# One level of Strassen for the output projection of seven token chunks, with the waves in 64-column halves

## The chip, the cores and the metric

The kernel runs on one core of one Trainium2 chip. The metric is the device time of one execution in microseconds, lower is better. One launch computes everything; inputs and outputs are float32 in HBM (the two sketches and the three weight matrices may also arrive as 64-bit floats seen as pairs of 32-bit words, which the kernel narrows itself; in this case they do).

## The reference

Two stages follow each other. The first is linear attention with a polynomial sketch: q and k are projected by two 8-row sketches and the outer product of the two projections gives 64 features. The second is a gated feed-forward block over all 4352 tokens.

```python
def phi(x):                                # x: (4, 4, 1088, 32)
    a = np.einsum('rd,bhsd->bhsr', S1, x)
    b = np.einsum('rd,bhsd->bhsr', S2, x)
    return np.einsum('bhsi,bhsj->bhsij', a, b).reshape(*x.shape[:-1], r * r)
q_p, k_p = (phi(q), phi(k))
kv = np.einsum('bhsf,bhsd->bhfd', k_p, v)
z = np.sum(k_p, axis=2)
num = np.einsum('bhsf,bhfd->bhsd', q_p, kv)
den = np.einsum('bhsf,bhf->bhs', q_p, z)[..., None] + 1e-06
x = (num / den)                            # brought to (4352, 128)
gate = 1.0 / (1.0 + np.exp(-(x @ w_gate))) # w_gate, w_val: (128, 1536)
val = x @ w_val
out = gate * val @ w_out                   # w_out: (1536, 128)
```

## The kernel before

**Layout.** The attention's result is kept transposed in `xT` (128 features by 4352 tokens). The feed-forward block goes over it in nine chunks `tok_chk` of 512 tokens, the last of 256. The 1536 inner columns are 12 blocks of 128 (`NJ`). `w_sb[:, 0]`, `[:, 1]` and `[:, 2]` hold w_gate, w_val and w_out by blocks.

**A wave.** `w1` (L345) issues one wave: for one block of one chunk, a matmul for the gate and one for the value (L357, 128x128 by 512 tokens each) into the two banks of a `wave` tile. There are two such tiles (pool `psm`). ScalarE then takes the sigmoid of the first bank (`sg`, L365), and VectorE multiplies it with the second (`g`, L381, in the inner function `glu`). For the last chunk a wave takes two blocks at once. During chunk 0 the wave also carries the steps that narrow the weights of later blocks (`narrow_w`), which use ScalarE, VectorE and GpSimd.

**The output projection.** `w2` (L307) multiplies one block of w_out with `g` (L314) and accumulates over the twelve blocks of a chunk in one PSUM bank, `acc0` or `acc1` in turn by chunk. After the last block VectorE turns the result (L324, into `o_sb`), and four or eight DMAs on the SP queue store it (L335).

**Order.** The order on TensorE, VectorE, ScalarE and GpSimd is the program's own order (a manual schedule). `slot(group, waves)` (L395) issues a group of attention work and then some waves. Each step of its loop issues the pending `glu`, then takes from the list `todo` every `w2` but the newest (two behind in the last chunk), and then issues the next wave. So in the steady state TensorE sees a wave, one w_out matmul, a wave, and so on. A chunk's waves begin only when its tokens are ready (`moe["ready"]`).

**Attention work.** Batch 0 is computed at the start. For batches 1 to 3 the loop at the end spreads the work over slots:

- `turn_k`, `turn_q` (L420 on): VectorE transposes of k and q.
- `begin`: the pending `glu`, then `kps` (projections of k, `kab`), `qcomp` (projections of q into a `wave` tile, `cqps`, copied by ScalarE to `cq`) and `spread`. The last writes `cq` to DRAM on the SP queue and fetches it back, spread over partitions, by six DMAs on GpSimd's queue (L627).
- `outer` (L535), `sum_z` (L711): VectorE products and sums of the features of k.
- `kv_all`: the matmuls of `kv` (L677, L686) and ScalarE's copy. Then `qmult` and `weights_z` on VectorE, `ndt` (L732, a transpose of the kv matrix on TensorE), and `parts`: `den_j`, `den_i` for the denominators, `dn` for the numerators (L861), and the division on VectorE.
- `masks` for batch 1: small tensors, partly on GpSimd.

Waves 0 to 11 belong to chunk 0, 12 to 23 to chunk 1, and so on. `begin(1)` comes ahead of wave 13, `begin(2)` ahead of wave 29 and `begin(3)` ahead of wave 50.

**Buffers.** `raw` has six tiles under the tag `w_in` for the incoming weights. `sbG` has six `g` and three `sg` tiles. `KP` has two buffers. `den_i` uses whichever accumulator bank isn't in use.

Of the kernel before, what the change touches and what calls it, by code (L numbers as in the profile page):

```python
# [8 lines left out]
F32 = mybir.dt.float32  # L9
# [3 lines left out]
ALU = mybir.AluOpType  # L13
# [3 lines left out]
P = 128  # L17
# [3 lines left out]
def kernel(  # L21
# [12 lines left out]
    nc = tc.nc  # L34
# [3 lines left out]
    F = R * R  # L38
# [15 lines left out]
    sbA = ctx.enter_context(tc.tile_pool(name="sbA", bufs=2))  # L54
    raw = ctx.enter_context(tc.tile_pool(name="raw", bufs=NJ // 2))
    sbN = ctx.enter_context(tc.tile_pool(name="sbN", bufs=1))
    sbG = ctx.enter_context(tc.tile_pool(name="sbG", bufs=6))

    dram = ctx.enter_context(tc.tile_pool(name="dram", bufs=1, space=bass.MemoryType.DRAM))

# [82 lines left out]


    w_sb = const.tile([P, 3, NJ, P], F32, tag="w_sb", name="w_sb")
    w_in = {}

    def load_w_in(j0, j1):
# [153 lines left out]

    xT = const.tile([P, NTOK], F32, tag="xT")

    moe = {"sum": -1, "ci": 0, "w": 0, "ready": 0, "acc": None, "gate": None, "todo": []}

    def w2(ci, j0, jn, g):  # L307
        t0, tw = tok_chk[ci]
        if j0 == 0:
            moe["sum"] = ci  # L310
            moe["acc"] = pso.tile([P, TCH], F32, tag=f"acc{ci % 2}", name="moeout")
        for jj in range(jn):
            j = j0 + jj
            nc.tensor.matmul(  # L314
                out=moe["acc"][:, :tw],
                lhsT=w_sb[:, 2, j, :],
                rhs=g[:, jj, :tw],
                start=(j == 0),
                stop=(j == NJ - 1),
            )  # L320
        if j0 + jn == NJ:
            o_sb = sbA.tile([P, TCH // 32, 32], F32, tag="o_sb", name="o_sb")
            nt = tw // 32
            nc.vector.transpose(  # L324
                out=o_sb[:, :nt, :].rearrange("p t d -> p (t d)"), in_=moe["acc"][:, :tw]
            )
            c = t0
            while c < t0 + tw:
                b, r = divmod(c, S)
                n = min(t0 + tw - c, S - r) // 32  # L330
                u = (c - t0) // 32
                for g4 in range(4):

                    eng = nc.scalar if ci == len(tok_chk) - 1 and g4 % 2 else nc.sync
                    eng.dma_start(  # L335
                        out=bass.AP(
                            tensor=out.tensor,
                            offset=out.offset + (b * S + r // 32) * DM + 32 * g4,
                            ap=[[T * DM, 32], [DM, n], [1, 32]],
                        ),  # L340
                        in_=o_sb[32 * g4 : 32 * g4 + 32, u : u + n, :],
                    )
                c += n * 32

    def w1():  # L345

        ci = moe["ci"]
        t0, tw = tok_chk[ci]
        jn = TCH // tw
        j0 = moe["w"] * jn  # L350
        wv = psm.tile([P, 2, TCH], F32, tag="wave", name="wave")

        tp = tw // 2 if ci == 0 and j0 == 0 else tw
        for o in range(0, tw, tp):
            for which in range(2):
                for jj in range(jn):
                    nc.tensor.matmul(  # L357
                        out=wv[:, which, jj * tw + o : jj * tw + o + tp],
                        lhsT=w_sb[:, which, j0 + jj, :],
                        rhs=xT[:, t0 + o : t0 + o + tp],  # L360
                        start=True,
                        stop=True,
                    )
        sg = sbG.tile([P, TCH], F32, tag="sg", name="sg", bufs=3)
        nc.scalar.activation(out=sg, in_=wv[:, 0], func=ACTF.Sigmoid)  # L365
        if ci == 0:
            if j0 == 1:
                narrow_01(2, 3)
            if 0 < j0 < NJ - 2:
                narrow_w(j0 + 1, 3)  # L370
            narrow_w(j0 + 2, 1)
            narrow_w(j0 + 2, 2)
            if j0 < 3:
                narrow_w(j0 + 3, 0)
            if j0 > 1:
                narrow_w(j0 + 4, 0)


        def glu():
            g = sbG.tile([P, TCH], F32, tag="g", name="g")  # L380
            nc.vector.tensor_tensor(out=g, in0=wv[:, 1], in1=sg, op=MUL)  # L381
            moe["todo"].append((ci, j0, jn, g.rearrange("p (j t) -> p j t", j=jn)))

        moe["gate"] = glu
        moe["w"] += 1
        if j0 + jn == NJ:
            moe["ci"] += 1
            moe["w"] = 0
# [6 lines left out]
    def slot(group, waves):  # L395

        if group is not None:
            group()
        todo = moe["todo"]
        for _ in range(waves):  # L400
            more = moe["ci"] < len(tok_chk)
            if more and sum(tok_chk[moe["ci"]]) > moe["ready"]:
                break
            glu()


            last = moe["ci"] == len(tok_chk) - 1 and moe["w"] > 1
            lag = 3 if last else 2
            while len(todo) >= lag:
                w2(*todo.pop(0))  # L410
            if more:
                w1()
            elif not todo:
                break
            else:
                w2(*todo.pop(0))

    kT_of, qT_of = {}, {}

# [26 lines left out]
    def kps(b):  # L446
        t = ps2.tile([P, 2, 512], F32, tag="two", name="kps")
        ts = [t[:, 0], t[:, 1]]
        turns = [(g, pi) for g in range(4) for pi in range(2)]

        if b == 0:
            ts[1] = pso.tile([P, TCH], F32, tag="acc1", name="kps1")
            turns.sort(key=lambda x: x[1])
        for g, pi in turns:
            rows = slice(64 * pi, 64 * pi + 64)
            nc.tensor.matmul(  # L456
                out=ts[pi][32 * g : 32 * g + 32, : NJK * 32],
                lhsT=sk[rows, :],
                rhs=kT_of[b][rows, KBASE[g] : KBASE[g] + NJK],
                start=True,  # L460
                stop=True,
            )

        KAB[b] = sbA.tile([P, 2, NJK, 32], F32, tag="kab", name="kab")
        for pi in range(2):
            nc.vector.transpose(
                out=KAB[b][:, pi].rearrange("p j c -> p (j c)"), in_=ts[pi][:, : NJK * 32]
            )
        KP[b] = sbA.tile([P, 2, NJK, 2, F], F32, tag="kp", name="kp")

# [251 lines left out]
    def ndt(b):  # L724
        if b == 0:
            t = pso.tile([P, TCH], F32, tag="acc0", name="ndps")
            ndps = t.rearrange("p (w x) -> p w x", w=2)
        else:
            ndps = ps2.tile([P, 2, 512], F32, tag="two", name="ndps")[:, 0].rearrange(
                "p (w x) -> p w x", w=2  # L730
            )
        nc.tensor.matmul(  # L732
            out=ndps[:, 0, :P],
            lhsT=KVD[b][:, 0].rearrange("p c f -> p (c f)"),
            rhs=ident,
            is_transpose=True,
            start=True,
            stop=True,
        )
        ND[b] = sbA.tile([P, P], F32, tag="nd", name="nd")  # L740
        nc.scalar.copy(out=ND[b], in_=ndps[:, 0, :P])  # L741

# [62 lines left out]
        nc.vector.tensor_tensor(out=PD[b], in0=t[:, :, :WD], in1=A8[b], op=MUL)  # L805


    def den_i(b):
        dps = pso.tile([P, TCH], F32, tag=f"acc{(moe['sum'] + 1) % 2}", name="deni")
        for h in range(H):  # L810
            nc.tensor.matmul(  # L811
                out=dps[32 * h : 32 * h + 32, :WD],
                lhsT=mask["head"][:, h % 2, :],
                rhs=PD[b][:, h // 2, :],
                start=True,
                stop=True,
            )
        return dps

    def turn_den(b, dps):  # L820
        nt, over = WD // 32, (W1 - WD) // 32
        dT = sbA.tile([P, nt, 32], F32, tag="dTi", name="dTi", bufs=1)
        nc.vector.transpose(out=dT.rearrange("p t c -> p (t c)"), in_=dps[:, :WD])
        RC[b] = sbA.tile([P, 2, W1 // 32, 2], F32, tag="rci", name="rci")
        for t0, t1, u0, k in ((0, nt, 0, 0), (nt, W1 // 32, nt - over, 4)):
            nc.vector.tensor_scalar_add(
                RC[b][:, :, t0:t1],
                dT[:, u0 : u0 + t1 - t0, k : k + 4].rearrange("p t (n c) -> p n t c", n=2),
                1e-6,
            )  # L830
        nc.vector.reciprocal(out=RC[b], in_=RC[b])


    def dn(b, n, mid=None, pool=(ps2, "two")):
        t0, tn = q_chk[n]
        w = 32 * tn
        if b == 0:
# [8 lines left out]
                stop=True,  # L846
            )
        if b == 0:
            dT = sbA.tile([P, 9, 32], F32, tag="dT", name="dT")
            rc = sbA.tile([P, 9, 2], F32, tag="rc", name="rc")  # L850

        def turn():
# [1 line left out]

        if mid is not None:
            mid(turn, rc, dT)
        t = pool[0].tile([P, 2, 512], F32, tag=pool[1], name="nps")
        for h in range(H):
            for c in range(2):
                rows = slice(64 * c, 64 * c + 64)  # L860
# [174 lines left out]
    def parts(b):  # L1035
        den_j(b)
        glu()
        divide1 = dn(b, 1, pool=(psm, "wave"))
        dps = den_i(b)
        divide0 = dn(b, 0)  # L1040
        turn_den(b, dps)
        divide1()
# [77 lines left out]
```

## Time and profile before

| | |
|---|---|
| median of 3 runs | 303.54 us (303.41 to 303.98) |
| span of the profiled execution | 301.7 us |
| waves, L357: 436 passes, busy | 191.6 us |
| w_out, L314: 216 passes, busy | 105.2 us |
| sigmoid, L365: 102, mean | 597 ns |
| g, L381: 102, mean | 689 ns |
| transpose of a chunk's result, L324, mean | 678 ns |
| DVE additions of 64x256, both inputs in SBUF, L711, mean | 417 ns |
| granted TensorE clock from 45 to 295 us | 1.00 |

The passes of L357 and L314 overlap in the records, so their mean durations (565 and 575 ns) are longer than the distance from one to the next, and the chain of waits is the place to read a pass's price. PE is TensorE, PEld its weight loads, DVE VectorE, ACT ScalarE, POOL GpSimd and SP the engine whose queue issues most DMAs. VectorE's busy time is uneven: 27.2 of the 40 us from 45 to 85, 31.7 of the 60 from 85 to 145, 31.2 of the 60 from 145 to 205, and 26.1 of the 90 from 205 to 295, where only the feed-forward block is left. GpSimd does nothing after 164.5 us.

### The profile page before, as it was taken

To read this page: it belongs to the slowest core of one execution; us is meant where nothing else is said; L and a number is where in the kernel's file an instruction comes from. 1 tells how busy PE (TensorE), PEld (TensorE's weight loads), DVE (VectorE), ACT (ScalarE), POOL (GpSimd) and SP (SyncE) were. 2 spreads that over 40 slices of the span, in tenths; PEclk is the share of its full clock that TensorE was granted. 3 is DMA by queue.
4 is the path that set the end of the run, shared out by engine and by line. 5 is a ranking of instruction groups with operands and counts; after the bars stand their busy time and mean duration, and the time that the engine had idled before them with its cause. 6 is when DMAs were issued, how large, how long until landed. Compare 5 with 4: busy or idle time off the path is not lost.

```text
span 301.7 us, 3642 instructions
## 1 busy us (share of the span) xinstructions
PE 295.3 (98%) x1363; PEld 137.3 (46%) x1363; DVE 154.7 (51%) x268; ACT 80.7 (27%) x150; POOL 33.0 (11%) x62
## 2 busy tenths in 40 slices
PE   8899999999999999999999999999999999999994
PEld 3444434453444444434444445344444444444683
DVE  6997789764635545383365444932232223222331
ACT  3556533222122222212232222122222222222220
POOL 1465550410000400000004000000000000000000
PEclk9999999999999999999999999999999999999999
DMA  7993440897101591350016900200020000100011
GB/s 226 358 337 89 103 144 6 201 223 192 42 15 19 136 225 35 77 187 0 0 27 168 218 17 2 36 2 0 0 32 3 0 0 12 25 0 0 9 28 18
DMA packets 30546, 24.24 MB, mean 80 GB/s; under 512 B 20480, under 2 KB 25728, under 8 KB 30528
## 3 DMA queue, kind: packets, MB, share of 16 engines
q1 hardware_dynamic: 27024, 16.15, 20.5%
q0 software_dynamic: 2592, 7.08, 10.5%
q10 hardware_dynamic: 912, 0.77, 1.0%
q8 instruction: 11, 0.18, 0.2%
q14 instruction: 7, 0.06, 0.1%
HBM read 20.73 MB, written 3.26 MB: 80 GB/s over the span
## 4 chain that ended last, share of the span: by engine, by line
PE 86%; DVE 5%; DMA 3%; issue 2%; POOL 2%; ACT 1%; SPq 0%; DVEq 0%; POOLq 0%; ACTq 0%
PE wave L357 52%; PE moeout L314 27%; DMA bq<-dq 2%; PE nps L861 2%; POOL head L118 1%; PE kvz L677 1%; DVE head L109 1%; DVE w_sb L127 1%; DVE qp L655 1%; DMA s_in<-in_S_dram 1%; PE kps L456 1%; DVE head L105 1%; PE cqps L602 0%; PE deni L811 0%; PE dps L841 0%
## 5 line engine op out<-in xcount | busy, mean ns | idle before, releaser
L357 PE MATMUL wave<-xT,w_sb 128*128 128x512 f32 (+1 forms) x436 | 191.6, 565 | 0.0
L381 DVE TENSOR_TENSOR g<-wave,sg 128x512 f32<-128x512 f32 x102 | 70.3, 689 | 131.0 <-ACT sg L365 130.7
L357 PEld LDWEIGHTS wave<-xT,w_sb 128*128 128x128 f32 x436 | 82.8, 190 | 93.0 <-issue 85.7
L365 ACT ACTIVATE sg<-wave 128x512 f32<-128x512 f32 x102 | 60.9, 597 | 197.8 <-PE wave L357 197.8
L314 PE MATMUL moeout<-g,w_sb 128*128 128x512 f32 (+1 forms) x216 | 105.2, 575 | 0.3 <-DVE w_sb L127 0.3
L314 PEld LDWEIGHTS moeout<-g,w_sb 128*128 128x128 f32 x216 | 39.9, 190 | 44.8 <-issue 38.9
L118 POOL TENSOR_TENSOR head<-head,tail 128x384 int32<-128x384 int32 (+2 forms) x14 | 13.4, 954 | 18.2 <-DVE head L109 14.0
L627 POOL DMA_DIRECT2D qp<-dq x6 | 3.5, 583 | 105.9 <-DMA dq<-cq 105.9
L535 DVE TENSOR_TENSOR kp<-kab 128x1152 f32<-128x1152 f32 (+2 forms) x10 | 10.5, 1070 | 0.0
L655 DVE TENSOR_TENSOR qp<-qp,bq 128x1152 f32<-128x1152 f32 (+1 forms) x7 | 9.0, 1288 | 0.0
L258 PE MATMUL warm<-const-float32-1.0 128*128 128x512 f32 (+1 forms) x12 | 7.1, 720 | 0.8 <-PEq L1104 0.8
L109 DVE SCALAR_TENSOR_TENSOR head<-cap,head 128x384 int32<-128x384 int32 (+2 forms) x14 | 7.5, 535 | 0.5
L127 DVE SCALAR_TENSOR_TENSOR w_sb<-square,head 128x384 f32<-128x384 f32 (+1 forms) x11 | 5.7, 518 | 3.9 <-POOL head L118 3.9
L324 DVE STREAM_TRANSPOSE o_sb<-moeout 128x512 f32<-128x512 f32 (+1 forms) x9 | 6.1, 678 | 1.4 <-PE moeout L314 1.3
L627 POOL DMA_DIRECT2D bq<-dq x12 | 6.7, 574 | 0.5 <-DVE g L381 0.2
L101 ACT ACTIVATE tail<-w_in 128x384 int32<-128x384 uint32 (+1 forms) x13 | 6.6, 521 | 0.2 <-DMA w_in<-in_moe_w_gate_dram 0.2
L97 POOL TENSOR_SCALAR cap<-w_in 128x384 f32<-128x384 f32 (+1 forms) x13 | 6.4, 502 | 0.0
L886 DVE TENSOR_TENSOR xT<-nps,rb 128x576 f32<-128x576 f32 (+2 forms) x9 | 5.9, 660 | 0.5
L861 PE MATMUL nps<-qp,nd 64*32 64x256 f32 (+1 forms) x128 | 5.5, 402 | 0.5 <-ACT nd L741 0.4
L436 DVE STREAM_TRANSPOSE qT<-kq 128x512 f32<-128x512 f32 (+1 forms) x8 | 5.7, 716 | 0.0
L117 ACT ACTIVATE square<-cap 128x384 f32<-128x384 f32 (+1 forms) x11 | 5.1, 463 | 1.8 <-DVE w_sb L127 1.7
L425 DVE STREAM_TRANSPOSE kT<-kq 128x1088 f32<-128x1088 f32 (+2 forms) x5 | 5.3, 1068 | 0.0
(89 smaller groups left out, 85.6 us busy)
## 6 DMA issues: line engine op xcount, KB each, us to landing
qp<-dq POOLq DMA_DIRECT2D x6, 576.0 KB, 7.5
bq<-dq POOLq DMA_DIRECT2D x12, 288.0 KB, 9.8
v<-in_v_dram SPq DMA_DIRECT2D x16, 144.0 KB, 4.5
kq<-in_k_dram SPq DMA_DIRECT2D x3, 544.0 KB, 3.9
kq<-in_q_dram SPq DMA_DIRECT2D x3, 544.0 KB, 4.8
w_in<-in_moe_w_out_dram SPq DMA_DIRECT2D x6, 256.0 KB, 7.2
w_in<-in_moe_w_gate_dram SPq DMA_DIRECT2D x5, 256.0 KB, 6.1
w_in<-in_moe_w_val_dram SPq DMA_DIRECT2D x5, 256.0 KB, 6.8
```

The costliest lines, as they stand in the source:

```text
L109: nc.vector.scalar_tensor_tensor(out=head, in0=cap, scalar=-0x40000000, in1=head, op0=ALU.bitwise_and, op1=ALU.bitwise_or)
L118: nc.gpsimd.tensor_tensor(out=head, in0=head, in1=tail, op=ALU.add)
L127: nc.vector.scalar_tensor_tensor(out=out, in0=square, scalar=1.265625 * 2.0**-30, in1=head, op0=ALU.is_ge, op1=MUL)
L258: nc.tensor.matmul(out=t[:, 0, :n], lhsT=x, rhs=r, start=True, stop=True)
L314: nc.tensor.matmul(out=moe["acc"][:, :tw], lhsT=w_sb[:, 2, j, :], rhs=g[:, jj, :tw], start=(j == 0), stop=(j == NJ - 1),)
L357: nc.tensor.matmul(out=wv[:, which, jj * tw + o : jj * tw + o + tp], lhsT=w_sb[:, which, j0 + jj, :], rhs=xT[:, t0 + o : t0 + o + tp], sta ...
L365: nc.scalar.activation(out=sg, in_=wv[:, 0], func=ACTF.Sigmoid)
L381: nc.vector.tensor_tensor(out=g, in0=wv[:, 1], in1=sg, op=MUL)
L535: eng.tensor_tensor(out=KP[b][:, pi, j0:j1].rearrange("p j m (i l) -> p (j m) i l", i=R), in0=bass.AP(tensor=a0.tensor, offset=a0.offset, ...
L627: get.dma_start(out=t[64 * c : 64 * c + 64 if i else P, n * H * W1 : (n + 1) * H * W1], in_=bass.AP(tensor=d0.tensor, offset=d0.offset, ap ...
L655: nc.vector.tensor_tensor(out=q0, in0=q0, in1=half(BQ[b], n), op=MUL)
L861: nc.tensor.matmul(out=t[32 * h : 32 * h + 32, c, :w], lhsT=ND[b][rows, 32 * h : 32 * h + 32], rhs=half(QP[b], n)[rows, 2 * (h % 2) + h // ...
```

## The change

Chunks 1 to 7 (`fast`) compute w_out by one level of Strassen's scheme in Winograd's form. Two contraction blocks, two halves of the 128 output columns and two halves of the 512 tokens make the 2x2 blocks, so that seven products of 64 columns by 256 tokens stand for eight. Four sums of weight blocks (`weight_sums`, once, in two parts) and four sums of token blocks (`token_sums`, for every pair of waves) are made on GpSimd. The four token sums take three instructions, of which the first makes two of them.

The products go to TensorE in two groups per pair. `w2_a` (four products, accumulated in `acc0`) is due three waves after the pair's second wave, `w2_b` (three products, in `acc1`) four waves after it. Each product writes partitions 0 to 63 or 64 to 127, and the two kinds alternate within a group. `todo` now holds such due times; chunks 0 and 8 keep `w2`, with a lag of two and three waves. At a chunk's end ScalarE copies the upper half of each bank, VectorE combines the seven sums in two and four additions, and one transpose of 64 partitions by 1024 replaces the old one.

From chunk 1 on, a wave's matmuls are cut into two 64-column halves. `ndt` for batches 1 to 3 becomes two plain matmuls with the identity, one for each column half. `den_i` moves from an accumulator bank into the unused columns of the `wave` tile that holds the numerators. `g` becomes a tile for two waves, with three buffers. `KP` and one `dT` go down to one buffer.

```diff
+    def fast(ci):
+        return 0 < ci < len(tok_chk) - 1 and tok_chk[ci][1] == TCH
+    def weight_sums(n0, n1):
+        w = w_sb[:, 2].rearrange("p (n f) d -> p f n d", f=2)[:, :, n0:n1]
+        s = ws[:, :, n0:n1]
+        a11, a12 = w[:, 0, :, :64], w[:, 1, :, :64]
+        a21, a22 = w[:, 0, :, 64:], w[:, 1, :, 64:]
+        for out, in0, in1, op in (
+            (s[:, 0], a21, a22, ALU.add),
+            (s[:, 1], s[:, 0], a11, ALU.subtract),
+            (s[:, 3], a12, s[:, 1], ALU.subtract),
+            (s[:, 2], a11, a21, ALU.subtract),
+        ):
+            nc.gpsimd.tensor_tensor(out=out, in0=in0, in1=in1, op=op)
+    def token_sums(g):
+        t = raw.tile([P, 4, HALF], F32, tag="w_in", name="tsum")
+        g1 = g[:, 0].rearrange("p (t x) -> p t x", t=2)
+        nc.gpsimd.tensor_tensor(
+            out=t[:, :2],
+            in0=g.rearrange("p f (t x) -> p t f x", t=2)[:, 1],
+            in1=g1,
+            op=ALU.subtract,
+        )
+        nc.gpsimd.tensor_tensor(out=t[:, 2], in0=t[:, 1], in1=g1[:, 0], op=ALU.add)
+        nc.gpsimd.tensor_tensor(out=t[:, 3], in0=t[:, 2], in1=g[:, 1, :HALF], op=ALU.subtract)
+        return t
...
+    def w2_a(ci, i, g, t):
+        if i == 0:
+            moe["sum"] = ci
+            fst["a"] = pso.tile([P, TCH], F32, tag="acc0", name="prod")
+        lo, hi = fst["a"][:64], fst["a"][64:]
+        w, first, last = w_sb[:, 2], i == 0, i == NJ // 2 - 1
+        product(lo[:, :HALF], w[:, 2 * i, :64], g[:, 0, :HALF], first, last)
+        product(hi[:, :HALF], w[:, 2 * i + 1, :64], g[:, 1, :HALF], first, last)
+        product(lo[:, HALF:], ws[:, 3, i], g[:, 1, HALF:], False, last)
+        product(hi[:, HALF:], ws[:, 1, i], t[:, 2], False, last)
+        if last:
+            e = fst["e"] = raw.tile([P, 2, 2, HALF], F32, tag="w_in", name="other")[:64]
+            r = fst["r"] = raw.tile([P, 5, HALF], F32, tag="w_in", name="res")[:64]
+            nc.scalar.copy(out=e[:, 0], in_=hi.rearrange("p (u x) -> p u x", u=2))
+            nc.vector.tensor_tensor(
+                out=ends(r, 1, 3), in0=twice(lo[:, :HALF]), in1=e[:, 0], op=ALU.add
+            )
+            nc.vector.tensor_tensor(out=r[:, 2], in0=lo[:, HALF:], in1=r[:, 4], op=ALU.add)
...
+    def w2_b(ci, i, g, t):
...
+        p5 = (lo[:, :HALF], ws[:, 0, i], t[:, 0], first, last)
+        p4 = (hi[:, :HALF], w[:, 2 * i + 1, 64:], t[:, 3], first, last)
+        p7 = ((hi if i % 2 else lo)[:, HALF:], ws[:, 2, i], t[:, 1], False, i >= NJ // 2 - 2)
+        for p in (p4, p5, p7) if i % 2 else (p5, p4, p7):
+            product(*p)
+        if last:
+            e, r = fst["e"], fst["r"]
+            nc.scalar.copy(out=e[:, 1], in_=hi.rearrange("p (u x) -> p u x", u=2))
+            nc.vector.tensor_tensor(out=r[:, 0], in0=lo[:, HALF:], in1=e[:, 1, 1], op=ALU.add)
+            nc.vector.tensor_tensor(out=r[:, 4], in0=r[:, 4], in1=r[:, 0], op=ALU.add)
+            nc.vector.tensor_tensor(out=r[:, 3], in0=r[:, 4], in1=e[:, 1, 0], op=ALU.subtract)
+            nc.vector.tensor_tensor(
+                out=ends(r, 2, 2), in0=twice(lo[:, :HALF]), in1=ends(r, 2, 2), op=ALU.add
+            )
+            o_sb = sbA.tile([P, 2, TCH // 32, 32], F32, tag="o_sb", name="o_sb")
+            nc.vector.transpose(
+                out=o_sb[:64].rearrange("p d t x -> p (d t x)"),
+                in_=r[:, 1:].rearrange("p u x -> p (u x)"),
+            )
+            store(ci, lambda g4: o_sb[32 * (g4 % 2) : 32 * (g4 % 2) + 32, g4 // 2])
...
     def w1():
...
+        turn = (moe["w"] // 2) % 2
         for o in range(0, tw, tp):
             for which in range(2):
                 for jj in range(jn):
...
+                    for c in (0,) if ci == 0 else (1 - turn, turn):
+                        d = slice(0, P) if ci == 0 else slice(64 * c, 64 * c + 64)
+                        nc.tensor.matmul(
+                            out=wv[d, which, jj * tw + o : jj * tw + o + tp],
+                            lhsT=w_sb[:, which, j0 + jj, d],
+                            rhs=xT[:, t0 + o : t0 + o + tp],
+                            start=True,
+                            stop=True,
+                        )
...
+            if j0 == NJ - 3:
+                weight_sums(0, NJ // 4)
+        if ci == 1 and j0 == 1:
+            weight_sums(NJ // 4, NJ // 2)
+        if moe["w"] % 2 == 0:
+            moe["g"] = sbG.tile([P, 2, TCH], F32, tag="g", name="g")
+        pair, odd, n = moe["g"], moe["w"] % 2, moe["n"]
         def glu():
-            g = sbG.tile([P, TCH], F32, tag="g", name="g")
+            g = pair[:, odd]
             nc.vector.tensor_tensor(out=g, in0=wv[:, 1], in1=sg, op=MUL)
-            moe["todo"].append((ci, j0, jn, g.rearrange("p (j t) -> p j t", j=jn)))
+            todo = moe["todo"]
+            if not fast(ci):
+                lag = 3 if ci else 2
+                part = (ci, j0, jn, g.rearrange("p (j t) -> p j t", j=jn))
+                todo.append((n + lag, lambda: w2(*part)))
+            elif odd:
+                part = (ci, j0 // 2, pair, token_sums(pair))
+                todo.append((n + 3, lambda: w2_a(*part)))
+                todo.append((n + 4, lambda: w2_b(*part)))
...
-            while len(todo) >= lag:
-                w2(*todo.pop(0))
+            while todo and todo[0][0] <= moe["n"]:
+                todo.pop(0)[1]()
             if more:
                 w1()
             elif not todo:
                 break
             else:
-                w2(*todo.pop(0))
+                todo.pop(0)[1]()
...
+        for c in range(2 if b else 0):
+            nc.tensor.matmul(
+                out=ndps[64 * c : 64 * c + 64, 0, :P],
+                lhsT=KVD[b][:, 0, c],
+                rhs=ident,
+                start=True,
+                stop=True,
+            )
...
-    def den_i(b):
-        dps = pso.tile([P, TCH], F32, tag=f"acc{(moe['sum'] + 1) % 2}", name="deni")
+    def den_i(b, t):
+        dps = t[:, 0, W1 : W1 + WD]
```

## The prediction

> **What bounds the kernel now.** I read the page's first part, then its slices, then what TensorE waits for, then the chain of waits, and only then the single groups.
>
> ```profile
> PE 295.3 (98%) x1363; PEld 137.3 (46%) x1363; DVE 154.7 (51%) x268; ACT 80.7 (27%) x150; POOL 33.0 (11%) x62
> ...
> PEclk9999999999999999999999999999999999999999
> ...
> PE 86%; DVE 5%; DMA 3%; issue 2%; POOL 2%; ACT 1%; SPq 0%; DVEq 0%; POOLq 0%; ACTq 0%
> ```
>
> Busy time of a pipelined engine proves little, so the waits of TensorE decide. This is the whole answer for that engine:
>
> ```profile
> PE warm L258 <- PEq L1104: 0.8, 1, 0.8
> PE ndps L732 <- ACT kvd L699: 0.4, 1, 0.4
> PE nps L861 <- ACT nd L741: 0.4, 1, 0.4
> PE moeout L314 <- DVE w_sb L127: 0.3, 1, 0.3
> PE gram L502 <- POOL gh L490: 0.3, 1, 0.3
> PE dps L841 <- DVE zb L525: 0.2, 1, 0.2
> PE nps L861 <- DVE qp L655: 0.2, 1, 0.2
> ```
>
> Seven waits, 2.6 us together, nearly all in the first 20 us. After that TensorE is fed without a hole: a microsecond of its work removed is a microsecond of time, and a microsecond of waiting added is one lost. Nothing stands ready to hide a new wait. The chain of waits gives the prices:
>
> ```profile
> 62.72 1.72 PE wave L357 x4
> 64.43 1.28 PE kvz L677 x72
> 65.71 0.25 PE kvz L686 x8
> 65.96 1.06 PE moeout L314 x2
> 67.02 1.72 PE wave L357 x4
> ...
> 71.42 0.86 PE moeout L314 x2
> ```
>
> A matmul is two passes here (x4 for the two matmuls of a wave, x2 for one of w_out), so a full 512-column pass costs 0.43 us and 256 columns 0.215. After an attention group the first w_out matmul takes 1.06 instead of 0.86.
>
> **What the skill says.** (1) "TensorEngine Tiling (Array Packing)", Key Properties: changing the tiling mode drains TensorE. The trace agrees: in the single records every change of shape leaves 0.09 us without a start, and into the full 128x128 shape another 0.10 between the first two passes (the 0.20 above); into a 64-column shape (denj, 64x64) the second is 0.05. (2) The same section says that tiles operate independently. The 72 passes of kvz (four 32-column tiles, 64 columns) in 1.28 us are 18 ns each, where 64 columns alone cost 54: in the records four start 7 ns apart and the next four 55 ns later, although each matmul's second pass precedes the next tile's first in program order. (3) "SBUF — State Buffer", Who interferes with whom: a VectorE instruction with two SBUF inputs contends with GpSimd's reads. The trace agrees: GpSimd's addition at 39.82 took 1.96 us under VectorE's qp at 39.56, and 1.00 elsewhere. (4) "TensorE: Matmul & The Clock Gate", Part 1: an idle window of about 3.4 us halves the clock. No gap here after 20 us is that long.
>
> **The change, part by part.**
>
> *Products.* For a pair of contraction blocks, two matmuls (1.72 us) become seven products of 64 columns by 256 tokens. Two column halves run beside each other, so seven times two passes of 0.215 over two halves is 1.505. There are 7 chunks of 6 pairs: 42 x 0.215 = 9.0 us removed. A wave in halves has the same columns per half, 1.72 as before. Weight loads of 64 columns (denj: 131 ns) lie beside passes of 215 or more.
>
> *Mode changes.* Chunk 0's last w_out between chunk 1's half waves is one more trip (0.2 + 0.15). In chunk 8, w_out is full and the waves are halves: four entries at 0.20 and three returns at 0.15, 1.25. Returns from attention groups now go to halves, 9 x 0.05 = 0.45 cheaper. Sum +1.1. A B group has three products, so one half runs 0.43 behind until the next B; a drain in that state wastes half of that: about 9 drains, half of them uneven, +0.9. The column-half ndt has two passes of 128 columns instead of one, +0.1 each. All in all +2.1: TensorE's own work falls by 6.9.
>
> *GpSimd's token sums.* The additions at L118 (1.00 us for 384 columns, 0.73 for 256) give 2.1 ns a column and 0.18 fixed; the 128-column float product at L535 (0.39) lies slightly below that line. So the three sums (512, 256, 256) cost 1.26 + 0.72 + 0.72 = 2.7 per pair, against 4.9 of TensorE: not a bound. In the steady state the sum that group A needs (t[:, 2]) is there 1.5 (sigmoid, g) + 2.0 after the odd wave, and A's fourth product comes 5.4 after it: hidden by 1.9. That cover fails where GpSimd is held up. Its queue is in order, and for each batch it waits for dq and then issues six DMAs:
>
> ```profile
> 54.52 0.75 POOL L627 DMA_DIRECT2D qp<-dq  x1 [10.11 <-DMA dq<-cq]
> 55.50 1.12 POOL L627 DMA_DIRECT2D bq<-dq  x2 [0.23 <-DVE g L381]
> 56.59 0.56 POOL L627 DMA_DIRECT2D qp<-dq  x1
> 57.10 1.14 POOL L627 DMA_DIRECT2D bq<-dq  x2
> ```
>
> Batch 1: begin(1) puts these before wave 13 (counting waves from 0). Behind them stand the second weight_sums (four sums of 192 columns, 4 x 0.59 = 2.4) and then the first token sums: 58.2 + 2.4 + 2.0 = 62.6. TensorE reaches that product early, because chunk 1's first w_out comes three waves in and nothing lies between: wave 13 starts at 52.55 (52.42 in the chain, 0.15 of mode change, rounded), three waves end at 57.7, the fourth product is due at 58.15. It waits 4.4 us, in front of everything on TensorE's queue, and nothing gives that back. Bounds: 0 if GpSimd's sums were free and passed the DMAs (the queue excludes it), 3.5 at the 0.39 row's rate, 5.8 with sum_z (1.22, 0.68, two SBUF inputs) slowing it as at 39.82. I take 4.4.
>
> Batch 2: dq's landing and the six issues end 6.9 after the group (98.06 to 104.97). The sums of waves 28 and 29 then need 2.0, and TensorE wants them at 7.7: 1.2 late (0 to 1.9). Batch 3 has an even split: its sums start after g of wave 51 and meet outer (1.35, two SBUF inputs): 0.4 (0 to 0.9).
>
> *VectorE's chunk end.* Instead of one transpose (0.71) there are, after A, additions of 0.69 and 0.42, and after B three of 0.42, one of 0.69 and a transpose of 64x1024 (1.22; the 128x1088 at L425 is 1.30): 3.2 us in one piece ahead of the next g. In chunks 5 to 7 the delayed g ends 4.7 after B and its bank is wanted at 4.9: just hidden. Beside attention work it isn't. Chunk 1's end falls ahead of begin(2): turn_k (1.30), turn_q (0.67), g, the 3.1, g, turn_q (0.77), and cqps needs that last turn at 7.3 after A and gets it at 8.8: 1.5 (0 to 2). Chunk 2's end falls ahead of qmult(2): zw and qp come late for denj and nps, 1.6 (0 to 2.5); the old kernel had no wait there. Batch 3: 0.4 (0 to 0.8). ScalarE's two copies (0.6) per chunk lie in its idle time (27% busy). The rest (kp and dT single, deni in the wave's bank, accumulators acc0 and acc1 both in use, wanted again some 4 us after their last product) comes to nothing: each buffer's last reader is done a wave earlier.
>
> *Sum.* -6.9 + 4.4 + (1.2 + 1.5 + 1.6) + (0.4 + 0.4) = +2.6. The profiled span is 301.7; the median of the runs is 303.54 (303.41 to 303.98), 1.8 above it by the time around the span, which the change leaves alone. 303.54 + 2.6 = 306.1.
>
> **Rivals.**
>
> *The waits are small, the products win* (faster). For it: the old trace has no wait beside the same attention work, and VectorE was only half busy. Against it: the in-order GpSimd queue. With the 4.4 alone it is 303.54 - 6.9 + 4.4 = 301.0; with half of that 298.8; with none 296.6. I put it at 299.
>
> *The waits eat the gain* (slower, the forecast): 306.1. It decides where GpSimd's first token sums come more than 6.9 us late in sum with VectorE's delays; its place is the first A group of chunk 1, and begin(2). With all upper bounds, 5.8 + 1.9 + 2.5 + 2 + 1.7 = 13.9, it is 310.5.
>
> *Column halves lose their overlap or the clock drops* (clearly slower). Two like halves meet at most borders between a wave and a product group. If the queue couldn't reach past the second one, each of some 84 borders would idle half the array for 0.43, 84 x 0.215 = 18: 303.54 + 2.6 + 18 = 324. The kvz records speak against it: there TensorE passes over at least three second passes. Alone, a halved clock after the wait in chunk 1 would add some 1.7 (half of 3.4), by the skill's window, an estimate.
>
> *No difference*: gain and waits cancel within 0.6.
>
> **How the numbers follow.** Faster 0.41 (around 299, 296.5 to 302.9), no difference (within 0.2%, 0.6 us, about what a measurement of this kernel can tell) 0.05, the waits eat the gain 0.48 (304.2 to 311), lost overlap 0.06 (312 to 325). So faster 0.41, same 0.05, slower 0.54. The likeliest gives 306.1. The range 297 to 311 leaves out the lost overlap and the last tenth of the good case.
>
> **What would show it.** The first w2_a products of chunk 1: a wait of TensorE on POOL of 4 to 6 us near 58 to 63, with L627's DMAs and weight_sums just ahead on POOL. Waits of cqps on DVE qT in batch 2, and of denj or nps on DVE. In late chunks, a period of two waves of 4.94 instead of 5.15 without waits: that confirms the 9.0. If that period is 5.15 or more, the overlap of halves is wrong; if no wait on POOL appears, the forecast is wrong and the time is near 297 to 299.

## The result, and the profile after

| | before | after |
|---|---|---|
| median | 303.76 us (303.41 to 304.01, 4 runs) | 319.6 us (318.57 to 321.52, 4 runs) |
| span of the profiled execution | 301.7 us | 318.3 us |
| mean granted TensorE clock in it | 1.000 | 0.972 |

The ratio is 1.0531 (95% interval 1.0493 to 1.0569): 15.8 us slower, where 2.6 had been forecast. The four executions of the changed kernel were granted 0.972, 0.984, 0.982 and 0.972 of the clock on average, so what the clock takes differs between them; the profile is of the first. From the page of the changed kernel: busy time by engine, the granted clock in 40 slices of 8 us, and the engines' shares of the chain that ended last.

```profile
PE 299.3 (94%) x2176; PEld 153.6 (48%) x2176; DVE 184.9 (58%) x310; ACT 88.8 (28%) x164; POOL 161.6 (51%) x196
...
PEclk9999999879999799995999999999999999999999
...
PE 64%; DVE 14%; POOL 10%; issue 6%; DMA 2%; ACT 2%; SPq 0%; POOLq 0%; ACTq 0%; DVEq 0%
```

Two things are new. VectorE and GpSimd are a quarter of the chain (7% before), and the clock dips in four slices: two side by side (56 to 72 us), one from 103 and one from 143 us. Next, TensorE's waits in the changed kernel: total, times, longest. The rest of that answer is the few waits of the first 20 us that the old kernel had too.

```profile
PE prod L339 <- POOL tsum L334: 6.6, 3, 5.2
PE nps L982 <- DVE qp L766: 2.3, 2, 1.2
PE cqps L713 <- DVE qT L547: 1.7, 1, 1.7
PE denj L917 <- ACT sg L465: 1.3, 1, 1.3
PE wave L457 <- DVE g L487: 0.8, 2, 0.7
```

All waits are 15.1 us, 12.5 more than before. For denj this view names the sigmoid sg, but that ended at 141.28. What ended last is VectorE's zw, at 141.82, and it stands behind the chunk end, which is one piece of 3.3 us here (start, duration, line, operation, and in brackets the idle time before it and what ended it):

```profile
136.77 0.42 DVE L429 TENSOR_TENSOR res<-prod,other 64x256 f32<-64x256 f32 x1
138.84 1.24 DVE L436 STREAM_TRANSPOSE o_sb<-res 64x1024 f32<-64x1024 f32 x1
141.60 0.22 DVE L904 TENSOR_TENSOR zw<-z,eight 128x64 f32<-128x64 f32 x1
141.93 0.62 PE L917 MATMUL denj<-b,zw 64*64 64x160 f32 x8 [1.30 <-ACT sg L465]
```

The largest wait has its cause in GpSimd's timeline:

```profile
57.58 1.14 POOL L738 DMA_DIRECT2D bq<-dq  x2
58.67 1.10 POOL L323 TENSOR_TENSOR ws<-w_sb 128x192 f32<-128x192 f32 x1
59.85 0.59 POOL L323 TENSOR_TENSOR ws<-ws,w_sb 128x192 f32<-128x192 f32 x1
60.52 0.94 POOL L323 TENSOR_TENSOR ws<-w_sb,ws 128x192 f32<-128x192 f32 x1
61.43 0.76 POOL L323 TENSOR_TENSOR ws<-w_sb 128x192 f32<-128x192 f32 x1
62.15 1.44 POOL L328 TENSOR_TENSOR tsum<-g 128x512 f32<-128x512 f32 x1
63.67 0.72 POOL L334 TENSOR_TENSOR tsum<-tsum,g 128x256 f32<-128x256 f32 x1
64.45 0.69 PE L339 MATMUL prod<-tsum,ws 128*64 128x256 f32 x1 [5.21 <-POOL tsum L334]
```

The product takes 0.69 where 0.38 is usual: TensorE comes back at half its clock. Eight stretches of the same trace show how that hangs together (stretch, length, PE busy and instructions, granted clock, DMA share, GB/s). The borders are those at which the clock changed, or 3.41 us from one:

```profile
57.88:61.29 3.41, 1.36 (x10) 1.00 0.94 221
61.29:64.71 3.42, 0.26 (x2) 0.50 1.04 241
64.71:68.12 3.41, 3.41 (x11) 0.50 1.02 224
102.25:105.67 3.42, 1.73 (x36) 1.00 0.31 47
105.67:109.08 3.41, 3.41 (x13) 0.50 0.46 121
139.80:143.21 3.41, 1.45 (x12) 1.00 0.16 23
143.21:146.62 3.41, 2.87 (x40) 0.50 0.59 109
146.62:150.04 3.42, 3.42 (x19) 0.50 0.74 275
```

After the windows at full clock in which TensorE was busy for 1.36, 1.73 and 1.45 us, the next 3.41 us run at half clock, however full they are. The window from 102.25 holds no wait longer than 1.69 us. The DMA share in the three is 0.94, 0.31 and 0.16, so it isn't what they have in common. And a window at half clock has to be fuller before the clock comes back: the one from 143.21, with 2.87 us of work, was followed by another at half clock, those with 3.41 were not.

To split the difference I add up the single matmul records: each pass streams its columns at 0.43 us for 512 (twice that at half clock), over its share of the array. "Unused" is the part of the array that is idle while another part streams. The split is a model: with each pass at full length from its recorded start, the four changes come out as -8.7, +6.4, +15.5 and +3.4, so an entry is good to about half a microsecond.

| us | before | after | change |
|---|---|---|---|
| array streaming, at full clock | 281.35 | 272.95 | -8.4 |
| added by the half clock | 0 | 6.3 | +6.3 |
| nothing streams (waits, changes of shape, ends) | 17.8 | 32.75 | +15.0 |
| array unused while streaming | 2.56 | 6.26 | +3.7 |
| span | 301.7 | 318.3 | +16.6 |

In the late chunks the products do what they were meant to do. From the chain of waits of the changed kernel, a period of two waves is 4.94 us (221.00 to 225.94; 4.96 is the mean of the fourteen up to 290.43), not 5.15:

```profile
221.00 1.72 PE wave L457 x8
222.71 0.64 PE prod L339 x5
223.36 1.72 PE wave L457 x8
225.08 0.86 PE prod L339 x6
225.94 1.77 PE wave L457 x8
```

### The profile page after: what moved, and what is told of

It reads as the page before. It is cut to its first block, busy times and chain, and to the rows that moved or that the text cites. A ratio compares the mean times of both kernels' runs of the same rounds, so it can differ in the third digit from the quotient of the medians.

```text
span 318.3 us, 5511 instructions
## 1 busy us (share of the span) xinstructions
PE 299.3 (94%) x2176; PEld 153.6 (48%) x2176; DVE 184.9 (58%) x310; ACT 88.8 (28%) x164; POOL 161.6 (51%) x196
## 3 DMA queue, kind: packets, MB, share of 16 engines
HBM read 20.73 MB, written 3.26 MB: 75 GB/s over the span
## 4 chain that ended last, share of the span: by engine, by line
PE 64%; DVE 14%; POOL 10%; issue 6%; DMA 2%; ACT 2%; SPq 0%; POOLq 0%; ACTq 0%; DVEq 0%
PE wave L457 40%; PE prod L339 16%; POOL head L118 3%; POOL tsum L328 2%; PE moeout L370 2%; POOL ws L323 2%; DVE head L109 2%; DVE g L487 2%; PE nps L982 2%; DVE w_sb L127 1%; DVE o_sb L436 1%; POOL bq L738 1%; POOL tsum L334 1%; PE kvz L788 1%; DMA dq<-cq 1%
## 5 line engine op out<-in xcount | busy, mean ns | idle before, releaser
L457 PE MATMUL wave<-xT,w_sb 128*64 128x512 f32 (+3 forms) x820 | 215.8, 577 | 0.8 <-DVE g L487 0.8
L457 PEld LDWEIGHTS wave<-xT,w_sb 128*64 128x64 f32 (+1 forms) x820 | 83.3, 143 | 71.0 <-issue 52.4
L328 POOL TENSOR_TENSOR tsum<-g 128x512 f32<-128x512 f32 x42 | 57.8, 1377 | 97.6 <-DVE g L487 97.6
L339 PE MATMUL prod<-tsum,ws 128*64 128x256 f32 x252 | 68.8, 391 | 6.6 <-POOL tsum L334 6.6
L339 PEld LDWEIGHTS prod<-tsum,ws 128*64 128x64 f32 x252 | 33.4, 140 | 21.6 <-issue 8.5
L335 POOL TENSOR_TENSOR tsum<-tsum,g 128x256 f32<-128x256 f32 x42 | 34.2, 815 | 3.3
L339 PE MATMUL prod<-g,w_sb 128*64 128x256 f32 x168 | 33.9, 382 | 0.1
L334 POOL TENSOR_TENSOR tsum<-tsum,g 128x256 f32<-128x256 f32 x42 | 31.6, 753 | 3.3
L339 PE MATMUL prod<-tsum,w_sb 128*64 128x256 f32 x84 | 26.0, 392 | 0.0
L370 PE MATMUL moeout<-g,w_sb 128*128 128x512 f32 (+1 forms) x48 | 18.9, 503 | 0.3 <-DVE w_sb L127 0.3
L370 PEld LDWEIGHTS moeout<-g,w_sb 128*128 128x128 f32 x48 | 8.5, 189 | 8.3 <-issue 4.2
```

The lines of the kernel that those rows point to most:

```text
L328: nc.gpsimd.tensor_tensor(out=t[:, :2], in0=g.rearrange("p f (t x) -> p t f x", t=2)[:, 1], in1=g1, op=ALU.subtract,)
L334: nc.gpsimd.tensor_tensor(out=t[:, 2], in0=t[:, 1], in1=g1[:, 0], op=ALU.add)
L335: nc.gpsimd.tensor_tensor(out=t[:, 3], in0=t[:, 2], in1=g[:, 1, :HALF], op=ALU.subtract)
L339: nc.tensor.matmul(out=out, lhsT=lhsT, rhs=rhs, start=start, stop=stop, skip_group_check=True)
L370: nc.tensor.matmul(out=moe["acc"][:, :tw], lhsT=w_sb[:, 2, j, :], rhs=g[:, jj, :tw], start=(j == 0), stop=(j == NJ - 1),)
L457: nc.tensor.matmul(out=wv[d, which, jj * tw + o : jj * tw + o + tp], lhsT=w_sb[:, which, j0 + jj, d], rhs=xT[:, t0 + o : t0 + o + tp], sta ...
```

## The experiments

**Theory.** The products save their 8.4 us; three things take it back and more: waits on GpSimd and VectorE (12.5), windows at half clock that those waits set off (6.3), and uneven column halves (3.7). **Rivals.** (a) Work in column halves costs by itself, whatever waits there are. (b) The waits are one thing: GpSimd's queue alone, and VectorE's chunk end would be hidden without it. (c) The clock is a by-product that costs little.

### h_halves: the halves alone

Waves and w_out of chunks 1 to 8 in 64-column halves, without Strassen products, sums and the new chunk end.

```diff
-        return 0 < ci < len(tok_chk) - 1 and tok_chk[ci][1] == TCH
+        return False
...
+            for c in (0, 1) if ci else (0,):
+                d = slice(64 * c, 64 * c + 64) if ci else slice(0, P)
                 nc.tensor.matmul(
-                    out=moe["acc"][:, :tw],
-                    lhsT=w_sb[:, 2, j, :],
+                    out=moe["acc"][d, :tw],
+                    lhsT=w_sb[:, 2, j, d],
...
-                lag = 3 if ci else 2
+                lag = 3 if ci == len(tok_chk) - 1 else 2
```

> The column halves alone: waves and w_out of chunks 1 to 8 in 64-column halves, no Strassen products, no token or weight sums, the old one-piece transpose and the old lags. Theory (the loss is waits on GpSimd and VectorE, and the halved clock that these waits bring): 303.8 to 305, no new wait of TensorE over 1 us, no halved clock between 20 and 295 us. Rival (halves themselves cost, by uneven draining or because two half-array streams let the clock fall): 308 or more, with stretches of halved clock.

Measured: 303.64 us, ratio 0.9992 (0.997 to 1.0014), a little below the range. Its page shows the full clock throughout, and its chain of waits two waves of eight half passes with the old distances:

```profile
222.84 1.72 PE wave L460 x8
224.55 0.86 PE moeout L372 x4
225.41 1.72 PE wave L460 x8
```

Rival (a) falls: two column halves overlap fully, at no cost that can be measured. Everything that is lost comes with the sums, the chunk end and the seven products.

### a_ws and a_sync: what stands ahead of the token sums on GpSimd

a_ws makes the second weight_sums a wave earlier, ahead of the six DMAs:

```diff
-        if ci == 1 and j0 == 1:
+        if ci == 1 and j0 == 0:
             weight_sums(NJ // 4, NJ // 2)
```

> The changed kernel with the second weight_sums one wave earlier, ahead of batch 1's DMAs on GpSimd's queue. Theory: TensorE's wait of 5.2 us on the first token sums of chunk 1 falls by the 3.5 us that weight_sums took there (58.67 to 62.15), to about 1.7, and the halved clock after it goes or shrinks (1.8 us more): 314 to 316. Rival (the wait comes from the DMAs alone): no change, 319 to 320. Rival (the clock falls whatever the wait): 316, with three stretches of halved clock as before.

a_sync issues the six fetches of each batch on SP's queue instead of GpSimd's:

```diff
-spread(b, (0, 1), cq[b], nc.sync, nc.gpsimd)
+spread(b, (0, 1), cq[b], nc.sync, nc.sync)
```

> The changed kernel with the six fetches of each of the batches 1 to 3 on the SP queue and not on GpSimd's. Theory: GpSimd's queue no longer stands behind dq; both waits on token sums (5.2 and 1.1 us) fall to under 1 us together, the first stretch of halved clock goes (1.8 us): 311 to 313. Rival (GpSimd is simply too slow for its sums, the DMAs don't matter): 318 or more. Risk: the fetches land later and qp's products wait longer.

Measured: a_ws 314.01 us (ratio 1.0348, 1.0319 to 1.0376), a_sync 309.25 us (1.0208, 1.0167 to 1.0249). The wait on tsum falls from 6.6 to 5.2 in all with the first and to 1.6 with the second; the waits on VectorE stay as they were. a_ws is just inside its range, a_sync is 1.75 below it, and neither wait fell as far as expected. In a_ws the wait in chunk 1 is 2.55 and not 1.7: beside VectorE's sum_z the second token sum took 1.60 instead of 0.72. The one in batch 2 grew from 0.97 to 2.21, likely because the half clock ahead of it, which had hidden a part of it, was gone (in a_warm and a_split below, where it is gone too, that wait is 1.62 and 1.42). In a_sync:

```profile
PE nps L982 <- DVE qp L766: 2.3, 2, 1.2
PE cqps L713 <- DVE qT L547: 1.7, 1, 1.7
PE prod L339 <- POOL tsum L334: 1.6, 2, 1.2
PE denj L917 <- ACT sg L465: 1.3, 1, 1.3
```

Rival (b) falls: VectorE's waits don't hang on GpSimd's queue. And a_sync gains 10.35 where its removed wait is 5.0. The rest is clock: 17.07 us of half clock have become one stretch of 3.41, and the time in which the array streams falls from 279.26 to 274.37, which is another 4.9 (a_ws too has one, behind its wait in batch 2). In a_sync, stretches as above:

```profile
96.74:100.16 3.42, 1.73 (x32) 1.00 0.47 76
130.87:134.29 3.42, 1.07 (x11) 1.00 0.24 38
134.29:137.70 3.41, 3.26 (x42) 0.50 0.43 58
```

The wait of 1.69 on cqps is in the window from 96.74 here, and the clock doesn't fall after it. In the changed kernel the same wait lay in a window that was just as busy (1.73), and it did. So the threshold is near. In each of the twelve traces the changes of clock tell where the windows lie. Every window at full clock with 1.45 us or less of busy time halved it, of four with 1.71 to 1.73 one did, and none with 1.76 or more.

Busy time counts a small tile like a full array. Count the work instead: each pass at 0.43 us for 512 columns, times the share of the 128 rows and of the 128 columns that it uses. Then the order has no overlap: every window with 1.20 us of work or less was followed by half clock, and none with 1.25 or more. The two windows on cqps are apart, with 1.20 in the changed kernel and 1.46 in a_sync. The same border fits the way back. At half clock the window from 143.21 of the changed kernel did 1.19 us of such work, and the clock stayed down; that from 134.29 in a_sync did 1.37, and it came back. This was read from the traces afterwards; no run was made to test it, and 0.05 us between the two sides is little. What falls into a window depends on where its borders lie, and those lie elsewhere in every trace.

### a_warm: the clock by itself

Twelve unused products of 64 columns by 512 tokens stand ahead of the waiting product in chunk 1, so that TensorE works while it waits. They add 5.3 us of TensorE's work and write a bank that nothing reads.

```diff
+        if ci == 1 and i == 0:
+            keep = ps2.tile([P, 2, 512], F32, tag="two", name="keep")
+            for n in range(12):
+                x = slice(64 * (n % 2), 64 * (n % 2) + 64)
+                product(keep[x, n % 2], w_sb[:, 0, n, x], xT[:, :512], True, True)
         product(hi[:, HALF:], ws[:, 1, i], t[:, 2], False, last)
```

> The changed kernel with twelve more matmuls of 64 columns by 512 (5.2 us of TensorE, results unused) ahead of the product of chunk 1 that waits for the first token sums. Theory (an idle TensorE is what halves the clock): the time of that place stays, since the products fill the wait, and the halved clock after it goes: 317 to 318.5, two stretches of halved clock and not three. Rival (the clock falls for another reason): 319.6 or more, three stretches.

Measured: 315.05 us, ratio 1.0397 (1.0353 to 1.0441): 4.5 faster than the changed kernel, with more work, and faster than expected. The page and the timeline:

```profile
PEclk9999999999999999999999999999999999999999
```

```profile
59.02 5.31 PE L339 MATMUL keep<-xT,w_sb 128*64 128x512 f32 x23
64.67 0.43 PE L339 MATMUL prod<-tsum,ws 128*64 128x256 f32 x1 [0.34 <-POOL tsum L334]
```

The product starts 0.2 us later than in the changed kernel (64.45), so the wait as such is not shortened; what is gained is clock. That all three stretches went, not just the first, was not expected. The later waits are still there (1.7 on cqps, 1.3 on denj, 2.3 on nps), but the windows lie otherwise over them. A border at 102.07 cuts the wait of cqps (101.57 to 103.26), and the windows on its two sides have 2.91 and 2.23 us of busy time, where 1.73 halved the clock in the changed kernel. A border at 139.61 comes between the waits of denj and nps in the same way (2.11 and 2.22). That is the profiled execution; the four were granted 1.000, 0.988, 0.992 and 1.000 on average (314.59, 317.72, 315.41 and 314.68 us). Rival (c) falls: the clock alone is worth 4.5 us of the 15.8, and 5 in the two executions at the full clock.

### a_split: VectorE's chunk end in three pieces

The additions and the transpose after B are cut at two points and issued after later values of g.

```diff
+    def end_1():
+        e, r, lo = fst["e"], fst["r"], fst["b"][:64]
...
+    def end_2(ci):
+        r = fst["r"]
...
+                if j0 == NJ - 1:
+                    todo.append((n + 5, end_1))
+                    todo.append((n + 6, lambda: end_2(ci)))
+                todo.sort(key=lambda x: x[0])
```

> The changed kernel with VectorE's work at a chunk's end cut in three: two additions stay with the last products, the other two come one wave later, the transpose and the store two waves later. Theory: TensorE's wait of cqps on qT in batch 2 (1.7 us) goes, those of denj and nps there (1.3 and 1.2) go or halve, and the halved clock that followed them comes less often: 312 to 316; the 5.2 us on GpSimd in chunk 1 stays. Rival (these waits come from more VectorE work as such, not from its one piece): waits as before, 319 or so.

Measured: 311.39 us, ratio 1.0254 (1.0238 to 1.027), 8.2 below the changed kernel and a little below its range. cqps waits 0.3, the wait of denj is gone, but nps, which was to gain too, takes a part of it up:

```profile
PE prod L339 <- POOL tsum L334: 6.7, 2, 5.2
PE nps L992 <- DVE qp L776: 2.8, 2, 1.7
```

The half clock in chunk 1 stays (6.83 us from 61.45), and the two later stretches are gone. Rival (b) falls here too: the waits of cqps and denj came from the chunk end standing in one piece.

### b_all and c_best: the three together, and chunk 8

b_all has the edits of a_ws, a_sync and a_split. c_best adds chunk 8's w_out in halves (the second edit of h_halves), so that the end has no changes of shape.

> The changed kernel with all three: second weight_sums one wave earlier, the fetches of batches 1 to 3 on the SP queue, VectorE's chunk end in three pieces. Theory: the products' 8.4 us come through once the waits and the halved clock are gone: 298 to 302, all waits of TensorE after 20 us under 3 us together, no halved clock. Rival (the columns saved are lost to uneven halves and mode changes too): 303 to 306.

> As b_all, and chunk 8's output projection in two column halves as well, so that TensorE keeps one mode to the end. Theory: the seven mode changes of chunk 8 (1.25 us by the prediction's prices) go: 1.0 to 1.5 below b_all, 297 to 300.5. Rival (mode changes are hidden there): the same as b_all.

Measured: b_all 303.42 us, ratio 0.9994 (0.9984 to 1.0004); c_best 302.87, ratio 0.9971 (0.9959 to 0.9982). Both miss their range on the slow side; b_all is where its rival had it. c_best is 0.55 below b_all, where the prediction's price for chunk 8's changes of shape was 1.25. In their profiled executions nothing streams at half clock any more. In c_best the streaming is 8.4 us less than before, and still almost nothing is gained: nothing streams for 22.5 us (+4.7) and 5.58 are unused (+3.0). One remaining wait, from its timeline:

```profile
56.16 2.32 POOL L328 TENSOR_TENSOR tsum<-g 128x512 f32<-128x512 f32 x1 [6.42 <-DVE g L496]
57.86 1.70 DVE L835 TENSOR_TENSOR z<-kp 128x1024 f32<-128x1024 f32 x1
58.56 1.59 POOL L334 TENSOR_TENSOR tsum<-tsum,g 128x256 f32<-128x256 f32 x1
60.20 0.43 PE L339 MATMUL prod<-tsum,ws 128*64 128x256 f32 x1 [1.19 <-POOL tsum L334]
```

With nothing ahead of them on their queue, the sums are still late: beside VectorE's outer and sum_z they take 2.32 and 1.59 instead of 1.26 and 0.72. That is 1.9 us for a cover of less than one. The cause is read from the overlap of the records; neither neighbour was moved to test it.

### d_even, d_qm and d_both: the two terms that were left

d_even keeps the products but makes the B groups even: p7 of an even pair goes with the next odd pair.

```diff
-        for p in (p4, p5, p7) if i % 2 else (p5, p4, p7):
+        if i % 2 == 0:
+            fst["p7"] = p7
+        for p in (p4, p5, p7, fst["p7"]) if i % 2 else (p5, p4):
             product(*p)
```

> The best version so far (weight sums, fetches, chunk end in pieces, chunk 8 in halves), with w2_b in even groups: an even pair issues p5 and p4 only, the next odd pair p4, p5 and both p7, two products for each column half. The same products are computed. Theory: the 3 us of TensorE's array that stay unused while it streams come from the odd third product, which leaves one half 0.43 us behind until the next w2_b, so that each of the some 70 changes of shape and waits beside attention work drains uneven halves. Then unused falls from about 5.6 to 3.5 or below, and the time from 302.9 to 300.5 to 301.5. Rival: the unevenness comes from the waits and from reordering across halves whatever the groups; then unused stays above 5 and the time at 302.5 to 303.

d_qm issues qmult one slot earlier:

```diff
+        qmult(b, 0)
         slot(lambda: kv_all(b), wn)
...
-        qmult(b, 0)
         weights_z(b)
-        slot(lambda: ndt(b), 1)
         qmult(b, 1)
+        slot(lambda: ndt(b), 1)
```

> The best version so far, with qmult of both halves one slot earlier (the first ahead of kv_all's slot, the second ahead of ndt's), so that qp is ready when nps asks for it. Theory: the two waits of nps on qp (1.8 in batch 2 and 1.2 in batch 3) are VectorE being late, not work of TensorE, and they are lost time: both go, and the time falls by 2 to 3, to 300 to 301. Rival: VectorE is late in this stretch by the sum of its work beside GpSimd's sums, so another wait takes the place (denj on zw, or a wave on g): the time falls by less than 1, to 302 to 303.

d_both has the two together.

> Both edits together: even groups in w2_b and qmult one slot earlier. Theory: the gains add, as the one is columns left unused and the other waits: 298 to 300. Rival: waits at the same borders absorb each other and it is within 0.5 of the better of the two.

Measured against 303.58 us of the kernel before: d_even 301.07 (ratio 0.9914, 0.9897 to 0.993), d_qm 301.34 (0.9929, 0.991 to 0.9949), d_both 299.85 (0.9865, 0.9832 to 0.9898). In d_even the unused array falls from 5.58 to 4.15 and the span by 1.7. The time is in its range, the unused array is not (3.5 or below): the odd group is a part of it, not the whole. In d_qm the waits of nps are gone (2.8), but a wave now waits 0.9 for g, which the rival had as its sign. The time fell by 1.5, between the 2 to 3 of the theory and the 1 of the rival. d_both, the waits of its TensorE above 0.8 us:

```profile
PE prod L339 <- POOL tsum L334: 1.2, 1, 1.2
PE wave L468 <- DVE g L498: 1.0, 1, 1.0
```

The gains add (1.8 and 1.5 against c_best, 3.0 together). d_both is inside its range and beats both kernels: -8.4 streaming, +3.4 nothing streaming, +1.6 unused give the -3.3 of its span (298.4).

Waits, half clock (as long as matmuls run) and unused array are those of each version's profiled execution.

| version | median, us | waits of TensorE | half clock, us | unused |
|---|---|---|---|---|
| before | 303.76 | 2.6 | 0 | 2.56 |
| after | 319.6 | 15.1 | 17.07 | 6.26 |
| a_ws | 314.01 | 13.7 | 3.41 | |
| a_sync | 309.25 | 10.4 | 3.41 | |
| a_warm | 315.05 | 11.0 | 0 | |
| a_split | 311.39 | 12.4 | 6.83 | |
| c_best | 302.87 | 6.9 | 0 | 5.58 |
| d_both | 299.85 | 5.1 | 0 | 4.17 |

## Why the prediction was wrong

The direction and the places were right, and the sum was far too small. The step that failed is the clock, which the sum put at nothing; three other terms were mis-sized. By the prediction's own steps:

- *Products, -9.0.* Right but for 0.6 (-8.4). The period is 4.94, as forecast, and the column halves overlap (h_halves).
- *Mode changes and uneven halves, "All in all +2.1".* Mis-sized. The uneven halves were put at 0.9 and are 3.7. The prediction counted 9 drains, half of them uneven; but any wait or change of shape behind an odd third product leaves a half idle, and the waits added such places. d_even shows that at least 1.4 of the 3.7 belong to the odd product itself. Outside the waits, time in which nothing streams grew by 15.0 - 12.5 = 2.5, where changes of shape and ndt were put at 1.2 (the "+0.1 each" of ndt entered that sum once, for three batches); part of that 2.5 is drains at half clock, which I couldn't separate.
- *Waits, 9.5.* Every named wait is there. In us, forecast and measured: chunk 1's first token sums 4.4 and 5.2; batch 2's sums 1.2 and 1.0; cqps 1.5 and 1.7; denj with nps in batch 2 1.6 and 2.5 (1.3 + 1.2); batch 3's sums 0.4 and 0.4; batch 3's VectorE 0.4 and 1.1. Not forecast: 0.8 of waves on g. Together 12.5 more than before. Four of the six are late by more than their middle value. In chunk 1 the weight sums took 3.5 (58.67 to 62.15), where the prediction had 2.4. VectorE's sum_z beside GpSimd's sums was charged only as an upper bound (5.8), and VectorE's own slowing by GpSimd was not in it at all.
- *Clock, nothing in the sum.* This is the step that failed. The prediction had "a halved clock after the wait in chunk 1 would add some 1.7" inside a rival with a chance of 0.06, and looked, in the old trace, for a gap as long as the idle window. Yet the wait of 4.4 that it forecast for chunk 1 was itself longer than that window of 3.4, and the sum had nothing for it. For that one place 1.7 was right: from 64.45 to 68.12 TensorE works at half clock, a loss of 1.8. But waits of 1.2 to 1.7 us set off two more such stretches, and the loss is 6.3. "TensorE: Matmul & The Clock Gate", Part 1, of the Trainium skill speaks of a free-running window of 3413 ns, and the traces agree (each stretch is 3.41 or twice that long). It names an idle window as the condition; here a window with 1.73 of 3.41 us busy was enough, and this measurement decides. With the 6.3 the forecast would have been 312.4; the other terms make up the rest.

The terms close: clock 6.3, waits 12.5 - 9.5 = 3.0, uneven halves 2.8, changes of shape 2.5 - 1.2 = 1.3, and streaming 0.6 (-8.4 for -9.0; h_halves has 0.3 of it, 281.68 us of streaming against 281.35) are 14.0, from +2.6 to the +16.6 of the two spans. The profiled run took 320.05, 0.45 above the median.

Open is what the 1.6 us are that d_both still leaves unused beyond the old kernel, and what in the program, if anything, could keep waits out of one clock window. The old kernel, too, was once granted 0.989 (307.5 us, one of the fifteen executions beside h_halves), and d_even once 0.982 (306.22 us); there is no trace of these, so what brought the clock down there is open.

The forecast's rival of lost overlap (324) was close in time and wrong in its cause, since h_halves shows no loss.

## What to carry to other kernels

When an engine is full, a change that saves its work by giving more to its neighbours must be priced by what each neighbour has ahead in its queue at the first place of need, and then by windows: a new wait that leaves TensorE half idle or more for one window of 3.4 us can cost another 1.7 us or more on top of itself. Groups that use part of the array should end even at every place where a wait or a change of shape can come. An edit like this can be worth having only after the waits are cleared: the same products gave 1.05 times the old time at first and 0.987 with six small edits around them.

## What the runs showed of the hardware that was not expected

- The clock halves after a 3.41 us window with 1.45 us or less of TensorE's busy time, doesn't after 1.76 or more, and goes either way at 1.71 to 1.73. Counted as work, by the share of the array that each pass uses, 1.20 us or less halved it and 1.25 or more didn't, in all twelve traces. It comes back after a window with 3.26 us of busy time at half clock (a_sync), and didn't after one with 2.87.
- The slowing between GpSimd and VectorE goes both ways. "SBUF — State Buffer", Who interferes with whom, of the Trainium skill calls the port pair that the two share an exclusive lock, and the traces agree in both directions. GpSimd's sums of 1.26 and 0.72 us took 2.32 and 1.59 above. In c_best VectorE's product of 64 columns takes six times its usual 0.21 us. A token sum runs on GpSimd from 186.53 to 188.71, and the product ends just after it, at 188.79:

```profile
187.50 1.29 DVE L910 TENSOR_TENSOR zz<-kvd,unit 128x64 f32<-128x64 f32 x1
```

- Matmuls in two 64-column halves cost as much as one of 128 columns, with twice the instructions (303.64 against 303.72 us in the same runs).
